# Attention and two feed-forward layers on one core: queries and keys in runs of 2304 bytes, three groups of rows in the down-sampled attention

## The chip, the cores and the metric

The kernel runs on one core of one Trainium2 chip. The metric is the time of one execution in device microseconds (us). Before the change it is 497.21 us, the median of three runs (494.74 to 502.7).

## What is computed

The reference, cut to what matters (batch 2, 8 heads, 576 tokens of 64 values a head; 1152 tokens of 512 values in the layers that follow):

```python
def _attn_ref(q, k, v):
    B, H, S, D = q.shape                       # 2, 8, 576, 64
    factor, Sd, scale = 4, S // 4, 1 / np.sqrt(D)
    q_d = q.reshape(B, H, Sd, factor, D).mean(axis=3)     # k_d, v_d alike
    out_d = sm_attn(q_d, k_d, v_d)             # softmax attention over 144 rows
    out_up = np.repeat(out_d, factor, axis=2)
    mask = np.abs(pos[:, None] - pos[None, :]) < factor
    attn = softmax(np.where(mask, scale * q @ k.T, -1e9))
    return out_up + attn @ v

def reference(...):
    x = attn_out.transpose(0, 2, 1, 3).reshape(B * S, H * D)        # 1152 x 512
    h = x @ w_in;  x = (h * np.tanh(softplus(h))) @ w_out           # 512 -> 2048 -> 512
    g = x @ w_gate; return (silu(g) * (x @ w_val)) @ w_out2         # 512 -> 1536 -> 512
```

## The kernel before

The attention works on pairs of heads: a pair's 2 x 64 values fill the 128 partitions, and there are 8 pairs (4 for each of two batches). `prep` (L476) loads a pair and turns it, `down` (L588) does its down-sampled attention, `load_windows` (L682) loads the value windows of the local attention, and `duo` (L717) does a third of the local attention of two pairs at a time (12 such calls). Its result, split in a high and a low part (`x_hi` on L274 or L272, `x_lo` L813), is the input `xy` of the first layer. The products of the layers run as three single products a chunk (high x high, high x low, low x high: L850, L851, L852, and L1144 to L1146 in the last layer); a product of the first layer for one chunk of 128 features and one third of the tokens is 12 of them.

In `prep` the queries and keys of a pair come by `ld_main` (L495): rows 0 to 511 in runs of 64 values (256 bytes), so that tile `qk` has row 4p + r of both heads on partition p. The last 64 rows of all 8 heads come once a batch by `ld_rem` (L469) into tile `qr`. TensorE turns `qk` in four transposes of 128x128 a matrix (L540) and `qr` in one of 64 rows (L551); ScalarE copies the result out into `qkT` (L557, L561), and VectorE adds four columns each into the down-sampled `qkd` (L568).

In `down` the 144 down-sampled rows of a head stand on 72 partitions in two groups, so that a pair has four groups: four score products (L605), a maximum a head (L610), four exponentials with their sums (L620), four multiplications by the reciprocals (L633 on ScalarE or L635 on VectorE), eight transposes (L644), two copies out (L272), and the products with the values (L656). The sums over the values, `vd` (L523), are GpSimd's.

The local attention of `duo` is: a mask product (L736), scores (L746), maximum and exponentials (L752 to L770), transposes (L776), value products (L789) and the sum with the repeated down-sampled result (L802).

The order of all of it is set by a planner (`Plan.run`). It goes through the program with a cost for each operation and, on each engine, takes the ready operation with the smallest due time; table `STEER` moves the due times of named groups. Where TensorE would have nothing ready, the planner puts a filler product `warm` (L1283, on a tile of zeros) into its order, up to 95 us of its own time. All DMAs are issued by SyncE's queue through one helper (L279), at most 6 under way. Each engine then runs its list in that order, with waits.

Of the kernel before, what the change touches and what calls it, by code (L numbers as in the profile page):

```python
# [62 lines left out]
}  # L63
KB = ()
COLD = 4.0


# [44 lines left out]
class Plan:  # L112
# [17 lines left out]
    def run(self):  # L130
# [10 lines left out]
        while todo:  # L141
            later, ran = [], False
            for e in names:
# [33 lines left out]
                if e == "DVE" and free["POOL"] > now:  # L177
                    d *= self.SHARE
# [1141 lines left out]
```

## Time and profile before

| | |
|---|---|
| runs | 502.7, 494.74, 497.21 us; median 497.21 |
| profiled execution, its own time | 495.21 us |
| its span, first to last instruction | 493.4 us |
| around the span | 1.8 us |
| TensorE busy | 483.1 us, 98% |
| VectorE, ScalarE, GpSimd busy | 327.3, 267.7, 21.5 us |
| mean granted TensorE clock | 0.993 |

A profile is one execution. Busy times count each instruction from start to end, and those of TensorE overlap, so that the time of a product is read from the distance between two starts, or from a piece of the chain of waits, which leaves overlaps out. The chain of waits goes back from the last instruction to what released each step. In views with windows, a DMA share of 1.00 means that all 16 DMA engines had work the whole time (a little above is an artefact of packets that overlap).

### The profile page before, as it was taken

To read this page: it belongs to the slowest core of one execution; us is meant where nothing else is said; L and a number is where in the kernel's file an instruction comes from. 1 tells how busy PE (TensorE), PEld (TensorE's weight loads), DVE (VectorE), ACT (ScalarE), POOL (GpSimd) and SP (SyncE) were. 2 spreads that over 40 slices of the span, in tenths; PEclk is the share of its full clock that TensorE was granted. 3 is DMA by queue.
4 is the path that set the end of the run, shared out by engine and by line. 5 is a ranking of instruction groups with operands and counts; after the bars stand their busy time and mean duration, and the time that the engine had idled before them with its cause. 6 is when DMAs were issued, how large, how long until landed. Compare 5 with 4: busy or idle time off the path is not lost.

```text
span 493.4 us, 9431 instructions
## 1 busy us (share of the span) xinstructions
PE 483.1 (98%) x3857; PEld 454.2 (92%) x3857; DVE 327.3 (66%) x634; ACT 267.7 (54%) x523; POOL 21.5 (4%) x41
## 2 busy tenths in 40 slices
PE   9999799999999999999999999999999999999996
PEld 6777589999999999999999999999998899998885
DVE  4989869639504643865578989798892298872522
ACT  3677668669627733867252775666661485730000
POOL 2333210000000000000000000000000000000000
PEclk9999979999999999999999999999999999999999
DMA  8999996622300640153111051423351042400022
GB/s 169 171 178 187 190 159 181 207 86 86 128 1 0 182 161 1 43 177 123 43 31 55 2 166 48 128 63 111 97 182 62 0 115 101 126 4 0 0 108 85
DMA packets 59993, 48.79 MB, mean 99 GB/s; under 512 B 32430, under 2 KB 55214, under 8 KB 59950
## 3 DMA queue, kind: packets, MB, share of 16 engines
q1 hardware_dynamic: 59950, 48.19, 38.0%
q8 instruction: 30, 0.49, 0.4%
q14 instruction: 13, 0.11, 0.1%
HBM read 45.83 MB, written 2.36 MB: 98 GB/s over the span
## 4 chain that ended last, share of the span: by engine, by line
PE 94%; DMA 4%; issue 1%; DVE 0%; SPq 0%
PE b L850 23%; PE b L852 23%; PE b L851 23%; PE b L1145 5%; PE b L1144 5%; PE b L1146 5%; DMA vw<-in_v_dram 3%; PE warm L1283 2%; PE b L789 2%; DMA qr<-in_k_dram 1%; PE b L540 1%; PE b L746 1%; PE b L605 1%; PE b L656 1%; PE b L776 1%; PE b L644 1%
## 5 line engine op out<-in xcount | busy, mean ns | idle before, releaser
L850 PE MATMUL b<-xy,wt 128*128 128x384 f32 x384 | 129.7, 338 | 0.0
L852 PE MATMUL b<-xy,wt 128*128 128x384 f32 x384 | 128.7, 335 | 0.0
L851 PE MATMUL b<-xy,wt 128*128 128x384 f32 x384 | 128.7, 335 | 0.0
L850 PEld LDWEIGHTS b<-xy,wt 128*128 128x128 f32 x384 | 72.3, 188 | 0.7 <-ACT cw L351 0.4
L851 PEld LDWEIGHTS b<-xy,wt 128*128 128x128 f32 x384 | 72.4, 189 | 0.0
L852 PEld LDWEIGHTS b<-xy,wt 128*128 128x128 f32 x384 | 72.3, 188 | 0.0
L852 PE MATMUL b<-G,wt 128*128 128x384 f32 x192 | 64.7, 337 | 0.0
L850 PE MATMUL b<-G,wt 128*128 128x384 f32 x192 | 64.6, 336 | 0.0
L851 PE MATMUL b<-G,wt 128*128 128x384 f32 x192 | 64.3, 335 | 0.0
L272 ACT ACTIVATE H<-b 128x384 f32<-128x384 f32 x60 | 29.3, 488 | 59.0 <-PE b L852 58.8
L358 DVE SCALAR_TENSOR_TENSOR cw<-raw,cw 128x512 uint32<-128x512 uint32 x68 | 46.5, 685 | 13.2 <-ACT cw L355 12.7
L351 ACT ACTIVATE cw<-raw 128x512 f32<-128x512 int8 x68 | 45.3, 667 | 17.9 <-DVE wt L372 12.5
L372 DVE TENSOR_TENSOR wt<-cw,wt 128x512 fp32r<-128x512 f32 x68 | 46.2, 685 | 5.5 <-ACT wt L272 4.0
L274 DVE CAST wt<-cw 128x512 fp32r<-128x512 f32 x29 | 12.3, 423 | 51.4 <-PE b L851 31.9
L355 ACT ACTIVATE cw<-cw 128x512 int32<-128x512 f32 x68 | 42.7, 628 | 1.0
L1145 PE MATMUL b<-wt,G 128*128 128x512 f32 x108 | 42.3, 392 | 0.0
L1144 PE MATMUL b<-wt,G 128*128 128x512 f32 x108 | 42.2, 391 | 0.0
L1146 PE MATMUL b<-wt,G 128*128 128x512 f32 x108 | 42.1, 390 | 0.0
L851 PEld LDWEIGHTS b<-G,wt 128*128 128x128 f32 x192 | 36.0, 188 | 0.0
L850 PEld LDWEIGHTS b<-G,wt 128*128 128x128 f32 x192 | 36.0, 188 | 0.0
L852 PEld LDWEIGHTS b<-G,wt 128*128 128x128 f32 x192 | 36.0, 188 | 0.0
L965 DVE TENSOR_TENSOR acc<-b,acc 128x384 f32<-128x384 f32 x36 | 19.6, 553 | 23.7 <-PE b L852 23.7
(108 smaller groups left out, 743.0 us busy)
## 6 DMA issues: line engine op xcount, KB each, us to landing
raw<-in_moe_w_out_dram SPq DMA_DIRECT2D x28, 512.0 KB
raw<-in_moe_w_in_dram SPq DMA_DIRECT2D x16, 512.0 KB
raw<-in_moe_w_gate_dram SPq DMA_DIRECT2D x12, 512.0 KB
raw<-in_moe_w_val_dram SPq DMA_DIRECT2D x12, 512.0 KB
vw<-in_v_dram SPq DMA_DIRECT2D x14, 189.0 KB
vq<-in_v_dram SPq DMA_DIRECT2D x8, 288.0 KB
out_dram<-acc SPq DMA_DIRECT2D x9, 256.0 KB
qk<-in_q_dram SPq DMA_DIRECT2D x8, 256.0 KB
```

The costliest lines, as they stand in the source:

```text
L272: ACT.activation(out, in_, AF.Copy)
L351: ACT.activation(cw.make(), raw.tile[:, 8:4104].bitcast(I8).rearrange("p (n b) -> p n b", b=8)[:, :, 0], AF.Prelu, scale=-1.0, bias=-56.0, ...
L355: ACT.activation(cw.tile.bitcast(I32), cw.tile, AF.Prelu, scale=-2.0 ** 27 / SLOPE, bias=-112 * 2.0 ** 27, alpha=SLOPE)
L358: DVE.scalar_tensor_tensor(out=cw.tile.bitcast(U32), in0=raw.tile[:, 0:4096].bitcast(U32).rearrange("p (n b) -> p n b", b=2)[:, :, 1], sca ...
L372: DVE.tensor_tensor(out=wt.tile[:, 1], in0=cw.tile, in1=wt.tile[:, 0].bitcast(F32), op=ALU.subtract)
L850: PE.matmul(out=ps, lhsT=wt_hi, rhs=m_hi, start=first, stop=False, **more)
L851: PE.matmul(out=ps, lhsT=wt_hi, rhs=m_lo, start=False, stop=False, **more)
L852: PE.matmul(out=ps, lhsT=wt_lo, rhs=m_hi, start=False, stop=last, **more)
L965: DVE.tensor_tensor(out=ya, in0=ps.tile[:, 0:n], in1=ya, op=ALU.add)
L1144: PE.matmul(out=ps.tile, lhsT=g[:, 0, tok], rhs=wt[:, 0], start=(f == fs[0]), stop=False)
L1145: PE.matmul(out=ps.tile, lhsT=g[:, 0, tok], rhs=wt[:, 1], start=False, stop=False)
L1146: PE.matmul(out=ps.tile, lhsT=g[:, 1, tok], rhs=wt[:, 0], start=False, stop=(f == fs[-1]))
```

## The change

Four edits in one:

- `ld_main` loads all 576 rows of a pair in runs of nine rows (9 x 64 values, 2304 bytes): partition 64h + n has rows 9n to 9n + 8 of head h. `ld_rem` and tile `qr` are gone.
- `turned` turns row r of the nine by a product of 64x64 with the identity for each head (each on its own 64 partitions), 9 x 2 a matrix. Eight of the nine fill one bank, and the ninth of both matrices shares another. The copies out write with a stride of nine elements. The local scores (`s_local`) now wait for all three copies, where two of three thirds had waited for two.
- `down` has three groups of rows on 128 partitions: the first 80 of the first head's 144 rows, its last 64 beside the first 64 of the second head, and the last 80 of the second head (the products of the first and third group write 128 rows, of which 80 are used). There are two score products of 128 rows and two of 64, a maximum over two groups and one over one, three exponentials, three multiplications, and three transposes for each half of the columns.
- The planner's costs are changed for these operations, VectorE's surcharge beside GpSimd falls on named operations alone (1.5 instead of 1.3 on all), and `STEER` is another table, so that the order on all engines is another.

```diff
 STEER = {
-    ('a', 0, 0, 0, 0, 0, 1): -4.2, ('a', 0, 1, 0, 0, 1, 1): 260.85, ('a', 0, 1, 2, 0, 1, 3): -48.85,
+    ('a', 0, 0, 0, 0, 0, 1): 60.95, ('a', 0, 1, 0, 0, 1, 1): 20.15, ('a', 0, 1, 2, 0, 1, 3): 181.55,
...
-KB = ()
+ROWS = 9
...
+        self.beside = Plan.SHARE if getattr(fn, "__name__", "") in Plan.SHARED else 1.0
...
-    REST, SHARE, REACH, LAND = 0.0, 1.3, 1.5, 0.5
+    REST, SHARE, REACH, LAND = 0.0, 1.5, 1.5, 0.5
+    SHARED = ("norm_l", "x_lo", "lo", "join")
...
-            dma(out=qr.tile[:, i], in_=(q, k)[i][b, :, 512:S].rearrange("h p d -> p h d"))
...
-                    dma(out=t.rearrange("p (r h d) -> p r h d", r=4, h=2), in_=src.rearrange("h (p r) d -> p r h d", r=4))
+                dma(out=qk.tile[:, i], in_=(q, k)[i][b, hs].rearrange("h (p r) d -> (h p) (r d)", r=ROWS))
...
+        def turned(t, z, i, r):
+            for h in range(2):
+                hh = slice(64 * h, 64 * h + 64)
+                PE.matmul(out=t[hh, NR * z:NR * z + NR], lhsT=qk.tile[hh, i, D * r:D * r + D], rhs=ident[hh, hh], start=True, stop=True)
...
-                        PE.transpose(out=t[:, 128 * r:128 * r + 128], in_=qk.tile[:, i, 128 * r:128 * r + 128], identity=ident)
+                for r in range(ROWS - 1):
+                    turned(t, r, i, r)
...
-                PE.transpose(out=t[:, 64 * i:64 * i + 64], in_=qr.tile[:, i, hs].rearrange("p h d -> p (h d)"), identity=ident[:64, :64])
+                turned(t, i, i, ROWS - 1)
...
+                    to = qkT.tile[:, j].rearrange("p (n r) -> p r n", r=ROWS)
+                    ACT.activation(to[:, 0:ROWS - 1] if i < 2 else to[:, ROWS - 1],
...
-            for c in range(2):
-                for h in range(2):
-                    hh = slice(64 * h, 64 * h + 64)
-                    PE.matmul(out=ba[h].tile[0:72, SD * c:SD * c + SD], lhsT=qkd.tile[hh, 0, 72 * c:72 * c + 72],
-                              rhs=qkd.tile[hh, 1, :], start=True, stop=True)
+            for h in range(2):
+                hh = slice(64 * h, 64 * h + 64)
+                PE.matmul(out=ba[h].tile[:, 0:SD], lhsT=t[hh, 64 * h:64 * h + 128], rhs=t[hh, SD:2 * SD], start=True, stop=True)
+            for h in range(2):
+                hh = slice(64 * h, 64 * h + 64)
+                PE.matmul(out=ba[0].tile[hh, SD:2 * SD], lhsT=t[hh, 80 * (1 - h):80 * (1 - h) + 64], rhs=t[hh, SD:2 * SD], start=True, stop=True)
+        rows = ((0, 80), (80, 128), (208, 80))
...
-            for h in range(2):
-                for c in range(2):
-                    ACT.activation(ed.tile[:, h, c], ba[h].tile[0:72, SD * c:SD * c + SD], AF.Exp, bias=md.tile[:, 0, h, c:c + 1],
-                                   scale=1.0 / 16.0, accum_out=md.tile[:, 1, h, c:c + 1])
+            for g in range(3):
+                ACT.activation(ed.tile[:, g], group(g), AF.Exp, bias=md.tile[:, 0, g:g + 1], scale=1.0 / 16.0, accum_out=md.tile[:, 1, g:g + 1])
...
-                for a in range(2):
-                    for c in range(2):
-                        PE.transpose(out=ba[h].tile[0:72, SD * a + 72 * c:SD * a + 72 * c + 72], in_=ed.tile[:, h, c, 72 * a:72 * a + 72],
-                                     identity=ident[:72, :72])
+                for g, (a, n) in enumerate(rows):
+                    PE.transpose(out=ba[h].tile[0:72, a:a + n], in_=ed.tile[0:n, g, 72 * h:72 * h + 72], identity=ident[:n, :n])
...
-            o1.append(add({E_PE: 0.36 if k else 0.48}, s_local(k), pr["evs"][:2 + (u == 2)] + [o_bf] + in_turn[-1:], w,
+            o1.append(add({E_PE: 0.36 if k else 0.48}, s_local(k), pr["evs"] + [o_bf] + in_turn[-1:], w,
```

What the new order does is seen at three places. SyncE's queue at the start of the program, before (`qr` is the tile of the last 64 rows, `qk` that of a pair, `vq` and `vw` the values):

```order
L279 DMA qr_100<-in_q_dram 64x8x64
L279 DMA qr_100<-in_k_dram 64x8x64
L279 DMA qk_134<-in_q_dram 128x8x64
L279 DMA qk_134<-in_k_dram 128x8x64
L279 DMA qk_143<-in_q_dram 128x8x64
L279 DMA qk_143<-in_k_dram 128x8x64
L279 DMA vq_152<-in_v_dram 72x4x256
```

The same queue in the changed kernel:

```order
L281 DMA qk_100<-in_q_dram 128x576
L281 DMA qk_100<-in_k_dram 128x576
L281 DMA qk_132<-in_q_dram 128x576
L281 DMA qk_132<-in_k_dram 128x576
L281 DMA qk_139<-in_q_dram 128x576
L281 DMA qk_139<-in_k_dram 128x576
L281 DMA vq_145<-in_v_dram 72x4x256
```

A pair's queries, which were the third transfer, are the first; each is 128 runs where it was 1024. In all, 106 rows of this queue stand where 111 did.

TensorE at its first down-sampled scores, before (`b` are the banks that products write):

```order
L540 MATMUL b_212<-ident,qk_143 128x128 x4
L551 MATMUL b_219<-ident,qr_100 128x64 x2
L1283 LDWEIGHTS wsrc
L1283 MATMUL warm<-wsrc 128x256
L605 MATMUL b_224<-qkd_198 72x144
L605 MATMUL b_225<-qkd_198 72x144
L605 MATMUL b_224<-qkd_198 72x144
L605 MATMUL b_225<-qkd_198 72x144
L540 MATMUL b_176<-ident,qk_143 128x128 x4
```

And in the changed kernel:

```order
L518 MATMUL b_250<-ident,qk_132 64x64 x16
L518 MATMUL b_268<-ident,qk_132 64x64 x4
L518 MATMUL b_152<-ident,qk_139 64x64 x16
L584 MATMUL b_174<-qkd_231 128x144
L584 MATMUL b_201<-qkd_231 128x144
L587 MATMUL b_174<-qkd_231 64x144 x2
L518 MATMUL b_210<-ident,qk_139 64x64 x16
L518 MATMUL b_250<-ident,qk_139 64x64 x4
```

Four transposes of 128x128 are now 16 products of 64x64, and a filler that stood ahead of the scores is gone. Over the program there are 55 fillers where there were 117 (12 where 26 stood at the start), and the turning is 288 products where it was 64 and 16 transposes.

TensorE just before the first product of the first layer, before (`pt` and `vw` are weights and values of the local attention, `exs` its exponentials, `xy` the layer's input, `wt` its weights):

```order
L789 MATMUL b_219<-pt_435,vw_270 64x32 x2
L789 MATMUL b_212<-pt_435,vw_270 64x32 x2
L776 MATMUL b_224<-ident,exs 128x128 x3
L605 MATMUL b_182<-qkd_234 72x144
L605 MATMUL b_193<-qkd_234 72x144
L850 MATMUL b_225<-xy_82,wt_734 128x384
L851 MATMUL b_225<-xy_82,wt_734 128x384
```

And in the changed kernel:

```order
L626 MATMUL b_174<-ident,ed_377 72x80
L626 MATMUL b_174<-ident,ed_377 72x128
L626 MATMUL b_174<-ident,ed_377 72x80
L717 LDWEIGHTS identb
L717 MATMUL b_210<-masks,identb 128x228
L727 MATMUL b_210<-qkT_209 32x38 x10
L727 MATMUL b_210<-qkT_209 32x35 x2
L831 MATMUL b_201<-xy_82,wt_997 128x384
L832 MATMUL b_201<-xy_82,wt_997 128x384
```

The first layer begins earlier, with more of the attention behind it: 72 of its products stood ahead of the last group of value products (L789) before, and 126 stand ahead of the last group of value products (L770) now. Behind that group both orders hold products of the layers alone.

## Rows read from the trace of the kernel before

**Rows 1.** The page: busy share of the engines, and the chain by engine.

```profile
PE 483.1 (98%) x3857; PEld 454.2 (92%) x3857; DVE 327.3 (66%) x634; ACT 267.7 (54%) x523; POOL 21.5 (4%) x41
...
PE 94%; DMA 4%; issue 1%; DVE 0%; SPq 0%
```

**Rows 2.** Windows: length, busy us of each engine, granted clock, DMA share, GB/s.

```profile
0.00:12.00 12.00, 10.95 (x75) 8.35 (x76) 4.96 (x13) 4.06 (x9) 3.24 (x17) 1.00 0.87 168
12.00:25.00 13.00, 12.07 (x282) 9.46 (x281) 11.70 (x36) 8.88 (x35) 4.25 (x6) 1.00 1.03 172
37.00:50.00 13.00, 12.70 (x321) 10.22 (x321) 12.46 (x36) 10.07 (x37) 4.45 (x6) 1.00 1.18 187
61.00:67.50 6.50, 6.50 (x79) 5.16 (x76) 2.98 (x10) 3.25 (x8) 2.17 (x3) 0.50 1.06 199
95.00:450.00 355.00, 355.00 (x1993) 348.60 (x1992) 239.12 (x407) 201.47 (x325) 0.00 (x0) 1.00 0.26 82
```

**Rows 3.** TensorE's timeline: start, us, instructions, and in brackets the idle time before.

```profile
16.92 0.33 PE L746 MATMUL b<-qkT 64*32 64x38 f32 x14 [0.93 <-issue]
30.71 0.88 PE L789 MATMUL b<-pt,vw 38*64 38x32 f32 x42 [1.03 <-DMA vw<-in_v_dram]
37.26 0.27 PE L551 MATMUL b<-ident,qr 64*128 64x64 f32 x1 [0.26 <-DMA qr<-in_k_dram]
53.83 0.57 PE L746 MATMUL b<-qkT 64*32 64x38 f32 x42 [0.69 <-issue]
59.17 0.59 PE L789 MATMUL b<-pt,vw 38*64 38x32 f32 x25 [2.15 <-issue]
66.19 0.69 PE L850 MATMUL b<-xy,wt 128*128 128x384 f32 x1
84.01 0.33 PE L851 MATMUL b<-xy,wt 128*128 128x384 f32 x1
87.83 0.34 PE L852 MATMUL b<-xy,wt 128*128 128x384 f32 x1
88.09 0.90 PE L789 MATMUL b<-pt,vw 38*64 38x32 f32 x48
```

**Rows 4.** The chain of waits in order of time: start, us, what.

```profile
1.05 5.55 PE warm L1283 x26
6.60 0.47 PE b L540 x4
9.29 0.44 PE b L540 x4
9.73 0.26 PE b L551 x2
10.21 0.65 PE b L605 x8
11.44 0.98 PE warm L1283 x9
37.53 0.37 PE b L644 x4
44.86 0.57 PE b L746 x46
48.86 1.53 PE b L789 x96
```

**Rows 5.** SyncE's queue in its timeline: start, us of issuing.

```profile
0.73 0.74 SPq L279 DMA_DIRECT2D qr<-in_q_dram  x1
2.19 0.63 SPq L279 DMA_DIRECT2D qk<-in_q_dram  x1
```

**Rows 6.** DMA issues: tile, count, KB of each.

```profile
qk<-in_q_dram SPq DMA_DIRECT2D x8, 256.0 KB
qr<-in_q_dram SPq DMA_DIRECT2D x2, 128.0 KB
```

**Rows 7.** Groups of the first 95 us: count, busy us, mean ns.

```profile
L620 ACT ACTIVATE ed<-b,md 72x144 f32<-72x144 f32 x32 | 11.6, 375 | 1.0 <-DVE md L615 0.9
```

More of the change, by code (lines that the diff above doesn't have):

```diff
@@ L177, in run @@
                 if e == "DVE" and free["POOL"] > now:
-                    d *= self.SHARE
+                    d *= o.beside
                 if o.table and table not in SERVED[o.table]:
@@ L264, in us_dma @@
     def us_dma(runs, size, engines=16, issue=None):
-        return [(issue or (0.35 + 0.0003 * runs), runs * (0.0224 if size <= 256 else 0.06 if size <= 1024 else 0.2) / engines, engines)]
+        return [(issue or (0.35 + 0.0003 * runs), runs * (0.0224 if size <= 256 else 0.06 if size <= 1024 else 0.118 if size <= 2304 else 0.2) / engines, engines)]
     def us_mm(n):
@@ L464, in keys @@
         return k0, k1, k0 - (BLK * t - 3)
-    pairs, rems = {}, {}
-    H_ = H
-    def ld_rem(b, i, qr):
-        def f(e):
-            if i == 0:
-                qr.make()
-            dma(out=qr.tile[:, i], in_=(q, k)[i][b, :, 512:S].rearrange("h p d -> p h d"))
-        return f
-    def prep(b, p, w):
-        qk = buf(ld, [128, 2, 512], F32, "qk", 3)
-        plan.at = ("r", b)
-        if p == 0:
-            qr = buf(ld, [64, 2, H_, 64], F32, "qr", 1)
-            l_r = []
-            for i in range(2):
-                l_r.append(plan.add({E_SP: us_dma(64 * H_, 256)}, ld_rem(b, i, qr), l_r, w - 12 - 9.04 + 2.71,
-                                    [] if l_r else [qr], [qr] if l_r else []))
-            rems[b] = (qr, l_r)
-        qr, l_r = rems[b]
+    pairs = {}
+    NR = S // ROWS
+    def prep(b, p, w):
+        qk = buf(ld, [128, 2, ROWS * D], F32, "qk", 3)
         vq = buf(ld, [72, 2, 2, 256], F32, "vq", 2)
@@ L498, in f @@
                     qk.make()
-                t, src = qk.tile[:, i], (q, k)[i][b, hs, 0:512]
-                if b in KB:
-                    dma(out=t.rearrange("p (h f) -> p h f", h=2), in_=src.rearrange("h (p r) d -> p h (r d)", r=4))
-                else:
-                    dma(out=t.rearrange("p (r h d) -> p r h d", r=4, h=2), in_=src.rearrange("h (p r) d -> p r h d", r=4))
+                dma(out=qk.tile[:, i], in_=(q, k)[i][b, hs].rearrange("h (p r) d -> (h p) (r d)", r=ROWS))
             return f
@@ L513, in prep @@
         for i in range(2):
[L514 removed]
+            l_q.append(plan.add({E_SP: us_dma(128, 2304)}, ld_main(i), l_q, w - 12, [] if l_q else [qk], [qk] if l_q else []))
         plan.at = ("v", b, p)
@@ L537, in f @@
                 t = ps[i].make()
-                for r in range(4):
-                    if b not in KB:
-                        PE.transpose(out=t[:, 128 * r:128 * r + 128], in_=qk.tile[:, i, 128 * r:128 * r + 128], identity=ident)
-                        continue
-                    for h in range(2):
-                        a = 256 * h + 64 * r
-                        PE.matmul(out=t[64 * h:64 * h + 64, 128 * r:128 * r + 128], lhsT=qk.tile[:, i, a:a + 64], rhs=ident,
-                                  start=True, stop=True)
+                for r in range(ROWS - 1):
+                    turned(t, r, i, r)
             return f
@@ L641, in f @@
                     ptd.make()
-                for a in range(2):
-                    for c in range(2):
-                        PE.transpose(out=ba[h].tile[0:72, SD * a + 72 * c:SD * a + 72 * c + 72], in_=ed.tile[:, h, c, 72 * a:72 * a + 72],
-                                     identity=ident[:72, :72])
+                for g, (a, n) in enumerate(rows):
+                    PE.transpose(out=ba[h].tile[0:72, a:a + n], in_=ed.tile[0:n, g, 72 * h:72 * h + 72], identity=ident[:n, :n])
             return f
@@ L649, in f @@
             def f(e):
-                copy(e, ptd.tile[:, h].rearrange("p a j -> p (a j)"), ba[h].tile[0:72, 0:2 * SD])
+                copy(e, ptd.tile[:, h], ba[h].tile[0:72, 0:2 * SD])
             return f
@@ L664, in down @@
         o = add({E_PE: 0.68}, score, o_d, w, ba + [ed, md], [qkd])
-        o = [add({"DVE": us_tt(2 * SD)}, mx(h), [o], w, use=[ba[h], md]) for h in range(2)]
+        o = [add({"DVE": us_tt((2 - h) * SD)}, mx(h), [o], w, use=[ba[h], md]) for h in range(2)]
         o = add({"DVE": 0.08}, neg, o, w, use=[md])
-        o = add({"ACT": 1.44}, exps, [o], w, use=ba + [md, ed], table="exp")
+        o = add({"ACT": 1.08}, exps, [o], w, use=ba + [md, ed], table="exp")
         o = add({"DVE": 0.3}, norm, [o], w, use=[md])
         o_e = []
+        x = [add({"ACT": (0.62, 0.31)[h], "DVE": (0.41, 0.21)[h]}, weigh(h), [o], w, use=[md, ed]) for h in range(2)]
         for h in range(2):
-            x = add({"ACT": 0.62, "DVE": 0.41}, weigh(h), [o], w, use=[md, ed])
-            x = add({E_PE: 0.3}, turn(h), [x], w, [] if h else [ptd], [ed, ba[h]] + ([ptd] if h else []))
-            o_e.append(add({"ACT": us_act(2 * SD, True)}, ev(h), [x] + o_e, w, use=[ba[h], ptd]))
+            o = add({E_PE: 0.32}, turn(h), x, w, [] if h else [ptd], [ed, ba[h]] + ([ptd] if h else []))
+            o_e.append(add({"ACT": us_act(2 * SD, True)}, ev(h), [o] + o_e, w, use=[ba[h], ptd]))
         o = add({E_PE: 0.68}, values, o_e + o_v, w, use=[vd, ptd, ba[0]])
```

43 lines of the change are left out of this document (21 added, 22 removed), and 50 rows, old and new, of the table STEER.

## The prediction

> **What bounds the kernel now.** I read the page first. TensorE is busy 98% of the span and 94% of the chain is its own work [rows 1]: whatever is saved must be saved in TensorE's list, as products that go or as time in which it had nothing useful to do. The windows say where that time is [rows 2]. From 95 us on TensorE is busy for all of the 355 us shown, at the full clock, and nothing that the change touches stands there. Before 95 us three things are mixed in: fillers (117 of them, of which the chain shows 26 in the first 5.55 us and 9 in 0.98 us [rows 4]), visible waits of 0.93, 1.03, 0.26, 0.69 and 2.15 us [rows 3], and a stretch from 61 to 67.5 us in which the granted clock is 0.50, the lower level of 1.2 GHz [rows 2]. That stretch follows the wait of 2.15 us, in which TensorE stood still. What TensorE waited for there is mostly data: the DMA share is 0.87 in the first 12 us and 1.03 to 1.18 behind them, at only 168 to 187 GB/s, whereas the stretch from 95 us on moves 82 GB/s with a share of 0.26, which would be 315 GB/s at a full share [rows 2]. The attention's transfers are small runs and fill the queues. VectorE is close behind (11.70 us busy of 13, 12.46 of 13 [rows 2]) and would be the next to end a wait.
>
> So the sum goes over TensorE's list up to the end of the attention, and the rest of the span is taken as it is.
>
> **The change, part by part.**
>
> Transfers. Queries and keys are 16 transfers of 256 KB and 4 of 128 KB [rows 6], together 4608 KB or 4.7 MB. At 172 GB/s with a share of 1.03 [rows 2], 167 GB/s at a full share, they take 28 us of full queues. No row shows runs of 2304 bytes beside small ones; the bounds are 28 us (no gain) and, at 315 GB/s, 15 us. I take 15, because the large runs of [rows 2] are of 1024 and 4096 bytes, on both sides of 2304. These 13 us are not on TensorE's list by themselves. They count through the waits below.
>
> The start. The first transposes begin at 6.60 us [rows 4], 4.4 us after the first pair's queries were issued at 2.19 us [rows 5]. These queries are now first in the queue, at the 0.73 us where `qr` stood [rows 5], so with the same 4.4 us the first products begin at 5.1 us: 1.5 us gained. The 12 fillers that are left there take 5.55 / 26 = 0.213 us each, to 3.6 us, and TensorE then waits 1.5 us. The bounds are 0 and the 3.0 us that 14 fillers took; 1.5 is the middle. The remaining 48 fillers that go took 0.98 / 9 = 0.109 us each [rows 4], 5.2 us. Together -6.7 us. This holds only if nothing else fills the gaps, which is what the next two terms are about.
>
> Turning. What goes: 64 transposes at 0.44 / 4 = 0.11 us, 7.0 us, and 16 at 0.26 / 2 = 0.13, 2.1 us [rows 4]; 9.1 us together. What comes: 288 products of 64x64, which in this number format are two passes each, as four products L605 are "x8" [rows 4]: 576 passes. No row shows such a pass. The nearest is L746, which also works on the two halves of the partitions in turn: 46 passes of 38 columns in 0.57 us, 0.0124 us each [rows 4], or 0.021 for 64 columns. L789 has 0.016 for 32 columns [rows 4], which is 0.032 if the columns count and 0.016 if it is a price of each pass. The lower end is L746's 0.0124 as it stands (7.1 us, -2.0), the upper end a pass as long as half of the 0.13 us of L551, 0.065 (37.4 us, +28.3). I take 0.021, from the row that is alike in its use of partitions: 12.1 us, +3.0 us.
>
> Here a rule speaks against the change: the Trainium skill, page "TensorEngine Tiling (Array Packing)", under "Gotcha 1: PSUM Pressure", says that different row tiles cannot access one PSUM bank at the same time. Both heads' products write one bank, so by that rule they would follow each other, and the term would be that of the second rival below. The trace speaks against it: L850 to L852 take (87.83 - 84.01) / 22 = 0.174 us for 384 columns [rows 3], 0.45 ns a column and so 17 ns for 38, and L746, whose two halves write one bank as well, takes 12.4 ns a pass.
>
> Down-sampled attention. On TensorE 64 transposes L644 at 0.37 / 4 = 0.0925 us [rows 4] become 48 of 80 or 128 columns; at the 0.11 us of the 128-column transposes that is 5.9 against 5.3 us, -0.6. The scores stay at four products of two passes a pair, 0.65 us for eight [rows 4]: 0 (up to +1.9 if a pass with 128 weight columns took 0.11 us). On ScalarE 8 of 32 exponentials with 0.375 us [rows 7] go, 3.0 us, and on VectorE shorter maxima. I cost both at nothing: TensorE's other work covers these engines now. The new wait of the local scores for the third copy also costs nothing as long as TensorE has another pair's work in hand; without that cover it is two small copies on ScalarE for each pair.
>
> Waits. With 13 us less in the queues, the wait of 2.15 us at 57 us should go, and with it the half clock: 6.5 us at 0.50 [rows 2] did the work of 3.2 us, so 3.3 us are lost there. Together -5.4 us. The four other waits, 2.9 us, I leave: with fewer fillers and a first layer that begins earlier, something will be late again, and VectorE is the first candidate. The bounds are 0 and -8.3 us.
>
> Sum: -6.7 + 3.0 - 0.6 - 5.4 = -9.7 us. Span 493.4 - 9.7 = 483.7 us; with the 1.8 us around it 485.5 us. The profiled execution took 495.2 us, 2.0 us under the median of the runs shown (497.2); the forecast is 2.0% under the one and 2.4% under the other. A measurement of this kernel can tell about 2% from no change.
>
> A second reading of the same sum, from the order: 54 more products of the first layer (126 instead of 72) stand ahead of the last group of value products. At 0.174 us they take 9.4 us, which then no longer stand behind it. So the span is 493.4 - 9.4 us plus whatever that group starts later than the 88.09 us of [rows 3]. By the sum it starts at 87.8 us. All that could make the forecast miss shows in that one time.
>
> **The rivals.**
>
> First, the waits stay: VectorE, full in half of the windows, ends the waits where DMA did, or the clock falls to its lower level again. Then the third gain is not there: 493.4 - 6.7 + 3.0 - 0.6 = 489.1, time 490.9 us. For it: 11.70 and 12.46 of 13 us busy. Against it: the change takes work off VectorE, and the longest wait came where transfers were late.
>
> Second, and slower: the two halves do not overlap, and each 64x64 pass loads its weights and streams them alone. At 0.065 us the turning costs +28.3 us: 493.4 - 6.7 + 28.3 - 0.6 - 5.4 = 509.0, time 510.8 us; at 0.050 it is 502.2 us. It decides from 0.038 us a pass on (9.1 + 12.7 us over 576), and 2% slower begins at 0.055. For it: 0.13 us for a product of 64 columns in L551, and the rule above. Against it: L746 and L789, both on quarters or halves of the array, at 12 to 16 ns.
>
> Third, a larger gain: all five waits and the half clock go (-8.3) and the turning costs 0.016 us a pass (+0.1): 493.4 - 6.7 + 0.1 - 0.6 - 8.3 = 477.9, time 479.7 us. For it: 13 us of queue time is more than all waits.
>
> Fourth, the change does not do what it says: runs of 2304 bytes take the queues as long as before. Then neither the start nor the waits gain: 493.4 - 5.2 + 3.0 - 0.6 = 490.6, time 492.4 us. Against it: 315 GB/s for large runs.
>
> **How the numbers follow.** Forecast 0.42, first rival 0.30, second 0.09, third 0.13, fourth 0.06. The range goes from the forecast with the lower end of the turning and without the four waits, 485.5 - 5.0 - 2.9 = 477.6, to the forecast with all waits and L789's 0.032 us, 485.5 + 5.4 + 6.2 = 497.1; rounded to 478 and 498 it leaves out most of the second rival. Faster by over 2% (under 487.3 us) are the third rival and three quarters of the forecast: 0.47 with a little of the first. Slower is most of the second rival, 0.07. The rest, 0.46, is within 2%.
>
> **What would show it.** In the profile of the changed kernel: first turning products at about 5.1 us; 32 passes of one matrix within 0.7 us (over 1.2 us would be the second rival); DMA share under 0.9 in windows between 12 and 50 us; no stretch of half clock between 50 and 70 us; the first product of the first layer by 50 to 56 us instead of 66.19; the last group of value products at 86 to 90 us. A wait of over 1 us on VectorE or ScalarE in TensorE's list behind 40 us would be the first rival, and a last group behind 98 us would make the forecast wrong altogether.

## The result, and the profile after

| | before | after |
|---|---|---|
| median of the runs | 496.95 us (20 runs) | 503.04 us (20 runs) |
| lowest and highest | 489.87 to 502.7 us | 497.31 to 510.29 us |
| ratio to before | | 1.0133, interval 1.0092 to 1.0175 |
| profiled execution | 495.21 us | 497.31 us |
| its span | 493.4 us | 495.5 us |
| its granted clock | 0.993 | 0.993 |

The changed kernel is 1.3% slower. A ratio leaves out runs that lie over 1.5% above the fastest of their kernel, so that it differs a little from the quotient of the two medians. The forecast was 485.5 us, in a range of 478 to 498 us: it had the wrong sign, and the measured time lies above the range.

The page of the profile after, its busy shares and its chain by engine and by line, answers to [rows 1]:

```profile
PE 486.1 (98%) x4275; PEld 457.3 (92%) x4275; DVE 325.0 (66%) x629; ACT 272.7 (55%) x504; POOL 21.5 (4%) x41
...
PE 98%; issue 1%; ACT 1%; DVE 0%
PE b L831 23%; PE b L833 23%; PE b L832 23%; PE b L1126 5%; PE b L1125 5%; PE b L1127 5%; PE b L518 4%; PE b L770 2%; PE warm L1264 2%; PE b L727 1%; PE b L637 1%; PE b L757 1%; PE b L626 1%; PE b L584 1%; PE b L587 1%
```

DMA, which had 4% of the chain, is gone from it. L518, the new turning, has 4% of 495.5 us, some 20 us, where the old one (L540) had 1%. The lines of the new kernel that matter here: L518 turning (on TensorE), L538 ScalarE's copies out of it (the old L557 and L561), L547 VectorE's sums for the down-sampled rows (the old L568), L1264 filler, L584 and L587 scores of the down-sampled attention, L626 its transposes, L727 local scores, L770 value products (the old L789), L831 to L833 products of the first layer (the old L850 to L852).

The windows after, with the columns of [rows 2] (length, busy us of PE, PEld, DVE, ACT, POOL, granted clock, DMA share, GB/s), the last one the half-clock stretch alone:

```profile
0.00:12.00 12.00, 10.93 (x223) 8.69 (x223) 3.72 (x11) 6.38 (x10) 4.78 (x20) 1.00 0.84 232
12.00:25.00 13.00, 10.71 (x277) 8.60 (x279) 8.67 (x28) 8.11 (x26) 2.74 (x4) 1.00 1.02 213
37.00:50.00 13.00, 12.00 (x260) 9.75 (x258) 7.07 (x21) 8.29 (x24) 2.17 (x3) 0.79 0.80 160
50.00:62.00 12.00, 11.85 (x321) 9.22 (x321) 11.21 (x33) 9.70 (x31) 4.46 (x6) 1.00 0.72 183
35.60:42.40 6.80, 6.80 (x97) 5.88 (x93) 3.64 (x8) 2.44 (x7) 2.17 (x3) 0.50 0.74 168
```

The half-clock stretch of the kernel before, in its full length:

```profile
60.90:67.70 6.80, 6.80 (x80) 5.46 (x77) 3.28 (x11) 3.25 (x8) 2.17 (x3) 0.50 1.05 198
```

The transfers did get better: between 37 and 50 us their share is 0.80 where it was 1.18. The runs of 2304 bytes took 15.4 us of the 16 engines (the sum over their packets), which is the 15 us that the prediction took. VectorE, which [rows 2] show nearly full (11.70 and 12.46 of 13 us), now has 8.67 and 7.07 us of work in the same windows: it waits. What VectorE waits for in the first 75 us (us in total, times, longest), before and after:

```profile
DVE qkd L568 <- ACT qkT L561: 3.3, 4, 2.1
```

```profile
DVE qkd L547 <- ACT qkT L538: 10.1, 7, 2.3
```

It waits for ScalarE's copies out of the turning. These, in the same 75 us (count, busy us, mean ns, then the idle time before and who ended it), before and after:

```profile
L557 ACT ACTIVATE qkT<-b 128x512 f32<-128x512 f32 x16 | 9.3, 592 | 9.8 <-PE b L540 9.7
```

```profile
L538 ACT ACTIVATE qkT<-b 128x512 f32<-128x512 f32 x16 | 17.2, 1095 | 13.6 <-PE b L518 13.5
```

Two things got worse here. ScalarE's wait for the turning grew from 9.7 to 13.5 us, and each of the 16 large copies takes 1095 ns instead of 592. And the half clock is not gone: 6.8 us at 0.50, as long as before, only 25 us earlier.

TensorE's timeline after (start, us, instructions, in brackets the idle time before):

```profile
3.72 1.66 PE L518 MATMUL b<-ident,qk 64*64 64x64 f32 x32
17.68 0.64 PE L727 MATMUL b<-qkT 64*32 64x38 f32 x48 [1.21 <-issue]
23.03 0.67 PE L626 MATMUL b<-ident,ed 80*72 80x80 f32 x6 [0.71 <-DVE m L747]
33.71 0.42 PE L770 MATMUL b<-pt,vw 38*64 38x32 f32 x13 [0.85 <-issue]
35.41 2.25 PE L518 MATMUL b<-ident,qk 64*64 64x64 f32 x40
64.14 0.45 PE L831 MATMUL b<-xy,wt 128*128 128x384 f32 x1
99.74 0.90 PE L770 MATMUL b<-pt,vw 38*64 38x32 f32 x48
```

The turning begins at 3.72 us, but the first layer at 64.14 us instead of 66.19 and the last group of value products at 99.74 us instead of 88.09 [rows 3].

In both kernels this stretch can be added up without a remainder, because TensorE is the bound: each product counts from its start to the next one's start, so that a wait behind it and a stretch of half clock are included. 109.0 us of both lists, from the first filler on:

| TensorE, us | before | after |
|---|---|---|
| fillers | 15.9 (117) | 8.3 (55) |
| turning | 10.6 | 21.9 |
| down-sampled scores | 5.7 | 7.9 |
| its transposes and value products | 10.7 | 10.5 |
| mask products, local scores | 11.7 | 12.1 |
| transposes, value products of `duo` | 19.1 | 15.2 |
| products of the first layer | 35.3 (193) | 33.1 (180) |

So at the end of it the changed kernel is 13 products of the first layer behind, at 0.174 us 2.3 us, and that is the 2.1 us by which its span is longer. The fillers gave 7.6 us, the turning took 11.3. The half clock falls on other products than before, and the waits stand behind other ones: of the turning's 21.9 us, 2.1 are lost to the half clock and 0.7 are a wait, and the lower sum of the value products (15.2 for 19.1) is almost all waits and half clock that lie elsewhere now. The account in the section on the prediction takes both out.

The chain of waits has the passes of the turning at full clock (start, us, what), which answers to [rows 4]:

```profile
5.71 1.31 PE b L518 x40
7.35 1.08 PE b L518 x32
9.29 2.25 PE b L518 x72
```

A pass costs 1.31 / 40 = 0.033, 1.08 / 32 = 0.034, 2.25 / 72 = 0.031 us. The forecast had 0.021.

### The profile page after: what moved, and what is told of

It is laid out like the page before. It is cut to its first block, busy times and chain, and to the rows that moved or that the text cites. A ratio compares the mean times of both kernels' runs of the same rounds, so it can differ in the third digit from the quotient of the medians.

```text
span 495.5 us, 10224 instructions
## 1 busy us (share of the span) xinstructions
PE 486.1 (98%) x4275; PEld 457.3 (92%) x4275; DVE 325.0 (66%) x629; ACT 272.7 (55%) x504; POOL 21.5 (4%) x41
## 4 chain that ended last, share of the span: by engine, by line
PE 98%; issue 1%; ACT 1%; DVE 0%
PE b L831 23%; PE b L833 23%; PE b L832 23%; PE b L1126 5%; PE b L1125 5%; PE b L1127 5%; PE b L518 4%; PE b L770 2%; PE warm L1264 2%; PE b L727 1%; PE b L637 1%; PE b L757 1%; PE b L626 1%; PE b L584 1%; PE b L587 1%
## 5 line engine op out<-in xcount | busy, mean ns | idle before, releaser
L831 PE MATMUL b<-xy,wt 128*128 128x384 f32 x384 | 129.7, 338 | 0.0
L833 PE MATMUL b<-xy,wt 128*128 128x384 f32 x384 | 128.6, 335 | 0.0
L831 PEld LDWEIGHTS b<-xy,wt 128*128 128x128 f32 x384 | 72.1, 188 | 0.7 <-ACT ed L604 0.2
L833 PEld LDWEIGHTS b<-xy,wt 128*128 128x128 f32 x384 | 72.1, 188 | 0.0
L833 PE MATMUL b<-G,wt 128*128 128x384 f32 x192 | 64.7, 337 | 0.0
L831 PE MATMUL b<-G,wt 128*128 128x384 f32 x192 | 64.6, 337 | 0.0
L274 ACT ACTIVATE H<-b 128x384 f32<-128x384 f32 x58 | 28.3, 488 | 54.0 <-PE b L833 53.7
L360 DVE SCALAR_TENSOR_TENSOR cw<-raw,cw 128x512 uint32<-128x512 uint32 x68 | 46.9, 693 | 11.0 <-ACT cw L357 10.6
L274 ACT ACTIVATE G<-H 128x1152 fp32r<-128x1152 f32 x14 | 16.0, 1164 | 38.7 <-PE b L1126 21.8
L831 PEld LDWEIGHTS b<-G,wt 128*128 128x128 f32 x192 | 36.0, 188 | 0.0
L833 PEld LDWEIGHTS b<-G,wt 128*128 128x128 f32 x192 | 36.0, 188 | 0.0
```

Source lines behind the costliest of these rows:

```text
L274: ACT.activation(out, in_, AF.Copy)
L360: DVE.scalar_tensor_tensor(out=cw.tile.bitcast(U32), in0=raw.tile[:, 0:4096].bitcast(U32).rearrange("p (n b) -> p n b", b=2)[:, :, 1], sca ...
L831: PE.matmul(out=ps, lhsT=wt_hi, rhs=m_hi, start=first, stop=False, **more)
L833: PE.matmul(out=ps, lhsT=wt_lo, rhs=m_hi, start=False, stop=last, **more)
```

## The experiments

Every ratio is to the kernel before, on the same chip. The changed kernel itself, run once more beside the three experiments that follow it, is the mark for them; the later ones ran on other chips, beside the kernel before alone.

### The changed kernel again

> The changed kernel once more, on the chip on which the variants run. List theory (the turning takes 0.033 us a pass in TensorE's list and all of it is paid): ratio to before 1.00 to 1.02. Clock theory (the median is longer than the profiled run because further stretches of half clock fall into most runs): its runs spread by 3.4 us steps with their mean granted clock, and the fewest such stretches go with the shortest time.

501.85 us, ratio 1.018 (1.0109 to 1.025); span 498.5 us at clock 0.993. Its half clock of 6.8 us lies at 45.7 to 52.5 us. The spread between its six runs goes with the clock: the one with 0.975 took 509.5 us, those with 0.993 took 500.3 and 500.36. But the first profile of the same kernel had 0.993 too, with a span of 495.5 us. The 3.0 us between them are waits: TensorE's add up to 7.3 us here and to 4.3 there, and one wait makes most of it (us in total, times, longest):

```profile
PE b L727 <- issue: 4.1, 1, 4.1
```

### Cheap turning, everything else as it is

```diff
-                for r in range(ROWS - 1):
-                    turned(t, r, i, r)
+                for r in range(4):
+                    PE.transpose(out=t[:, 128 * r:128 * r + 128], in_=qk.tile[:, i, 128 * r:128 * r + 128], identity=ident)
...
-                turned(t, i, i, ROWS - 1)
+                PE.transpose(out=t[:, 128 * i:128 * i + 128], in_=qk.tile[:, i, 448:576], identity=ident)
```

> The changed kernel with its order as it is, but the turning left out: in its place transposes of 128x128 as long as those of before (10 for each pair's matrices instead of 36 products), so the values are not the reference's. List theory: 576 passes at 0.033 us (19.0 us) become 80 transposes at 0.11 us (8.8 us), and the time falls by 8 to 11 us under the changed kernel, to 0.99 to 0.995 of before. Waits theory (the turning is hidden by waits, and the loss is in waits that moved): less than 3 us.

490.23 us, ratio 0.994 (0.9897 to 0.9984), 11.6 us under the changed kernel beside it. The same loads, the same order, the same copies; only TensorE's passes are others, 80 transposes that took 11.6 us of the list instead of 21.9. Its timeline, ScalarE's large copies in the first 75 us, and its stretch of half clock:

```profile
55.22 0.45 PE L831 MATMUL b<-xy,wt 128*128 128x384 f32 x1
90.85 0.90 PE L770 MATMUL b<-pt,vw 38*64 38x32 f32 x48
```

```profile
L538 ACT ACTIVATE qkT<-b 128x512 f32<-128x512 f32 x16 | 17.1, 1109 | 7.5 <-PE b L526 7.3
```

```profile
29.90:36.70 6.80, 6.80 (x59) 4.73 (x58) 4.00 (x9) 4.91 (x12) 2.06 (x3) 0.50 1.02 157
```

Both marks come back by 8.9 us, and ScalarE's wait for the turning falls from 13.5 to 7.3 us. The price of the passes stands on the path, nearly one for one. What does not go with it: TensorE's waits behind the first product still add up to 3.4 us (4.3 in the changed kernel), and the half clock is as long as in the other two.

### The passes doubled

```diff
                 PE.matmul(out=t[hh, NR * z:NR * z + NR], lhsT=qk.tile[hh, i, D * r:D * r + D], rhs=ident[hh, hh], start=True, stop=True)
+                PE.matmul(out=t[hh, NR * z:NR * z + NR], lhsT=qk.tile[hh, i, D * r:D * r + D], rhs=ident[hh, hh], start=True, stop=True)
```

> Each turning product is issued twice, with the same result; order otherwise as in the changed kernel. List theory: another 576 passes at 0.033 us, 16 to 20 us more than the changed kernel. Waits theory: under 8 us, since fillers and waits stand beside them.

518.29 us, ratio 1.0518 (1.0448 to 1.0588): 16.4 us over the changed kernel for 576 more passes, 0.029 us each. With the experiment above this is a slope in both directions.

### The short runs again

```diff
-        qk = buf(ld, [128, 2, ROWS * D], F32, "qk", 3)
+        qk = buf(ld, [128, 2, ROWS, D + 1], F32, "qk", 3)
...
-                dma(out=qk.tile[:, i], in_=(q, k)[i][b, hs].rearrange("h (p r) d -> (h p) (r d)", r=ROWS))
+                dma(out=qk.tile[:, i, :, 0:D], in_=(q, k)[i][b, hs].rearrange("h (p r) d -> (h p) r d", r=ROWS))
```

A row of 65 values on the partition keeps the destination from being one piece, so that each transfer is 1152 runs of 256 bytes.

> The changed kernel with queries and keys landing in rows of 65 values, so that each transfer is 1152 runs of 256 bytes again; order and products as in the changed kernel. Transfer theory (the long runs are worth what the forecast put on them): first products 1 to 3 us later and 5 to 10 us more time. List theory (TensorE's list decides, the transfers had room): within 3 us of the changed kernel.

505.74 us, ratio 1.0251 (1.0187 to 1.0314), 3.9 us over the changed kernel. The DMA queue in the first 62 us (packets, MB, share of 16 engines), of the kernel before, of the changed one and of this one:

```profile
q1 hardware_dynamic: 32007, 11.00, 103.3%
```

```profile
q1 hardware_dynamic: 17511, 11.86, 85.3%
```

```profile
q1 hardware_dynamic: 31684, 10.73, 105.3%
```

The queues are full again and move less, and it costs some 4 us: that is what the long runs are worth here (the two intervals overlap, 1.0109 to 1.025 and 1.0187 to 1.0314, so the size is rough). It lies between the two expectations, and below the 5.4 us of waits and half clock that the prediction drew from the transfers.

### One pass, measured by itself

A small kernel without the attention (its output is zeros, and it leaves out the whole computation) issues rows of products behind fillers at full clock. Two of its loops:

```python
for z in range(24):
    for h in range(2):      # L43: the halves in turn, one bank; L47: a bank each
        PE.matmul(out=banks[0][hs[h], 64 * (z % 8):64 * (z % 8) + 64], lhsT=qk[hs[h], 0, 64 * (z % 9):64 * (z % 9) + 64], rhs=ident[hs[h], hs[h]], start=True, stop=True)
for z in range(48):         # L50: one half only
    PE.matmul(out=banks[3][hs[0], 64 * (z % 8):64 * (z % 8) + 64], lhsT=qk[hs[0], 0, 64 * (z % 9):64 * (z % 9) + 64], rhs=ident[hs[0], hs[0]], start=True, stop=True)
```

> No attention and no layers: TensorE alone, in blocks of 48 like products with 30 fillers between them, and zeros as output. Bank theory (two row tiles in one bank follow each other): 64x64 products of both halves into one bank 0.033 us a pass, into two banks clearly less, 0.015 to 0.022; all on one half 0.033. Streaming theory (a pass of 64 columns costs its columns whatever the bank): 0.029 to 0.035 in all three. Tile theory (64x32 tiles overlap and 64x64 tiles do not): products of 32 weight columns at 0.012 us for 38 moving columns and at 0.015 to 0.020 for 64. Scores with 128 weight columns and 144 moving columns 0.10 to 0.115 us a pass, with 72 weight columns 0.08.

TensorE's timeline of it (start, us from the first start to the last end, shapes of weight tile and operand, count of passes):

```profile
14.62 3.01 PE L43 MATMUL b<-ident,qk 64*64 64x64 f32 x96
20.95 3.02 PE L47 MATMUL b<-ident,qk 64*64 64x64 f32 x96
27.27 5.81 PE L50 MATMUL b<-ident,qk 64*64 64x64 f32 x96
36.39 1.06 PE L55 MATMUL b<-qk 64*32 64x38 f32 x96
40.77 1.54 PE L60 MATMUL b<-ident,qk 64*32 64x64 f32 x96
57.12 5.40 PE L70 MATMUL b<-ident,qk 128*128 128x128 f32 x48
75.14 6.15 PE L78 MATMUL b<-qk 64*128 64x144 f32 x96
84.61 6.10 PE L82 MATMUL b<-qk 64*64 64x144 f32 x96
```

A block's time is counted to the start of the filler behind it (17.57 us for L43, 23.89 for L47, 33.01 for L50, 37.39 for L55, 42.24 for L60, 62.36 for L70). So a pass of 64 columns is 59.8 ns when all go to one half (L50), 30.7 ns when two halves take turns (L43), and 15.4 ns when four tiles of 64x32 do (L60). A pass is thus equally long on its tile in all three, some 60 ns, and as many run beside each other as there are different tiles in turn. L55 is the form of the row that the prediction scaled, L746: four tiles, 10.4 ns. The turning has two. None of the three theories came out as written: one bank or two is the same, one half alone is twice as long, and tiles of 64x64 overlap as those of 64x32 do. Against transposes of 128x128 (L70, 109 ns), 72 passes of 30.7 ns a pair replace 10 transposes, 2.2 against 1.1 us. A product with 128 weight columns is no dearer than one with 64 when its like stand in a row (L78, L82). The count of tiles is not the whole price, though: the value products L789 also go to four tiles in turn (two halves of the rows, two of the columns), with 32 columns, and take 16 ns a pass [rows 4], as much as L60 with 64 columns. What sets that was not tried.

### Every filler twice

```diff
             PE.matmul(out=wtile[:, 0:256], lhsT=wsrc[:, 0:128], rhs=wsrc[:, 0:256], start=True, stop=True)
+            PE.matmul(out=wtile[:, 0:256], lhsT=wsrc[:, 0:128], rhs=wsrc[:, 0:256], start=True, stop=True)
```

> The changed kernel with every filler issued twice, so 110 products where 55 are. Clock theory (fewer fillers are why the clock falls oftener): the mean granted clock of its runs rises from 0.985 to that of the kernel before (0.990) or above, and the time grows by less than the 6 us that 55 fillers take, or falls. List theory alone: mean clock as in the changed kernel, and 4 to 7 us more time.

505.23 us, ratio 1.016 (1.0103 to 1.0217). The clock of its runs is 0.995 in the mean, against 0.985 over 26 runs of the changed kernel and 0.987 over the 11 runs of before beside it. That is what the clock theory wanted. More fillers go with a higher clock, then, but what they give back they cost: the ratio stays near that of the changed kernel (1.0133 and 1.018 on other chips).

### Four groups of rows again

The changed kernel with the `down` of the kernel before, in two orders: with the table as it stands the planner puts in 130 fillers, and with a table made for it 76 (the changed kernel has 55).

> The changed kernel with the down-sampled attention of before (four groups of 72 rows); its order is the planner's for these operations with the same table, so the order moves as well. If the three groups are worth something (fewer exponentials on ScalarE): 2 to 6 us slower than the changed kernel. If they cost what their scores cost on TensorE (1.5 us): 1 to 3 us faster.

> The changed kernel with the four groups of rows of the kernel before in its down-sampled attention, this time with an order planned for it (76 fillers instead of 55, against 130 in the attempt before). If the loss lies in the turning and the groups are worth little, it comes within 3 us of the changed kernel: a span of 494 to 501 us, a ratio of 1.00 to 1.02. If the three groups with their 128 weight columns are part of the loss: a span under 493 us, a ratio under 0.997. If the three groups gain what the attempt before showed: a ratio over 1.025.

In this order they took 513.73 us, ratio 1.0375 (1.0281 to 1.047), and 507.94 us, ratio 1.0225 (1.0118 to 1.0332). The first lies in no range that was expected, and says little, since 75 fillers more are in it. The second has its span, 498.5 us, in the range of the first theory, and its ratio just above it. In the second, L600 is the old exponential; before it, the changed kernel's:

```profile
L604 ACT ACTIVATE ed<-b,md 128x144 f32<-128x144 f32 x24 | 8.7, 375 | 2.5 <-DVE md L600 2.5
```

```profile
L600 ACT ACTIVATE ed<-b,md 72x144 f32<-72x144 f32 x32 | 11.5, 370 | 3.1 <-DVE md L595 3.1
```

Three groups do save their 3 us of ScalarE, and nothing shows them as the main cause of the loss: without them the time is not lower in either order. Whether they gain the half per cent between 1.018 and 1.0225 can't be told; the intervals overlap and the orders differ.

### The right price in the planner

```diff
-            o = plan.add({E_PE: (0.56 if i < 2 else 0.15)}, t_main(i) if i < 2 else t_rem,
+            o = plan.add({E_PE: (1.06 if i < 2 else 0.27)}, t_main(i) if i < 2 else t_rem,
```

with a table found for it, 20 fillers.

> The changed kernel itself with one difference: the costs of the turning products in the planner are 1.06 and 0.27 us instead of 0.56 and 0.15, and the steering table is one found for these costs, so that the start holds 20 fillers instead of 55 and another order. The turning passes are as dear as in the changed kernel. If the order was made for a price that is too low and that is what costs, 35 fillers at 0.109 to 0.15 us (4 to 5 us) go and waits behind the passes go with them: a span of 487 to 492 us, a ratio of 0.985 to 0.997. If the price of the passes alone makes the loss, the fillers' place is taken by waits: a span of 494 to 498 us, a ratio of 1.005 to 1.02.

505.6 us, ratio 1.0268 (1.019 to 1.0346), slower than both theories. Waits took the fillers' place, as the second theory said, and more, 10.7 us instead of 4.3; the largest:

```profile
22.78 0.71 PE L638 MATMUL b<-ptd,vd 72*64 72x144 f32 x8 [1.89 <-issue]
37.47 0.98 PE L728 MATMUL b<-qkT 64*32 64x35 f32 x47 [3.46 <-issue]
44.58 0.65 PE L638 MATMUL b<-ptd,vd 72*64 72x144 f32 x6 [1.77 <-issue]
```

The planner priced the turning at half of what it takes; but that this made the order bad is not borne out by this one other order.

### Four quarters instead of two halves

If tiles in turn are what counts, queries and keys on different halves give four tiles of 64x64. Two attempts: queries on the lower and keys on the upper 64 partitions (two half-width transfers, the code below), and queries as they were with the keys' heads swapped by two transfers of 64 partitions. Both need a fourth bank and share one new order with 72 fillers.

```diff
-                dma(out=qk.tile[:, i], in_=(q, k)[i][b, hs].rearrange("h (p r) d -> (h p) (r d)", r=ROWS))
+                dma(out=qk.tile[64 * i:64 * i + 64], in_=(q, k)[i][b, hs].rearrange("h (p r) d -> p h (r d)", r=ROWS))
...
+            for i, h in ((0, 0), (1, 1), (0, 1), (1, 0)):
+                ii = slice(64 * i, 64 * i + 64)
+                PE.matmul(out=ps[p0 + i].tile[64 * h:64 * h + 64, NR * z:NR * z + NR], lhsT=qk.tile[ii, h, D * r:D * r + D],
+                          rhs=ident[ii, ii], start=True, stop=True)
```

> The changed kernel with queries on the lower and keys on the upper half of the partitions (still in runs of 2304 bytes, both heads side by side), so that the turning products go to four quarters of the array in turn instead of two; in this form the order of the start had to be planned anew (72 fillers instead of 55). Tiles in flight: four tiles in turn cost 15.4 ns a pass in the small kernel, so 576 passes take 8.9 us instead of the 21.9 us of the changed kernel's list, and some 13 us less in the list, minus 2 to 3 us for the 17 more fillers, gives a span of 485 to 489 us, a ratio of 0.975 to 0.99. Rival, 64x64 tiles overlap no more than two at a time whatever their number (30.7 ns a pass, 17.7 us): a span over 493 us, a ratio of 0.995 to 1.01. In the profile, 32 passes in a row take 0.5 us by the first and 1.0 us by the second.

> The attempt with four quarters again, in the same order on TensorE, with the queries landing on all 128 partitions as in the changed kernel and the keys in two transfers of 64 partitions that swap the two heads, so that the four products of a row again go to four quarters. In the attempt before, 64 passes in a row took 1.16 us (18 ns each) but the runs of 2304 bytes took 164 ns each at the median, against 93 in the changed kernel, and the list stood 17 us more than before in waits and half clock. If the loss there came from the way in which its transfers land on 64 partitions, the runs come back towards 93 ns (at least for the queries), the waits of 3.9 and 3.8 us go, and the span is 485 to 492 us, a ratio of 0.98 to 0.995. If the four quarters themselves or this order cost what was lost, the span stays over 500 us, a ratio over 1.015.

511.66 us, ratio 1.0348 (1.0272 to 1.0424), and 508.75 us, ratio 1.0318 (1.0277 to 1.0358): both are slower than the changed kernel (1.0133 and 1.018). The first lies in neither of its two ranges, the second in the rival's. The timeline of the second attempt:

```profile
19.68 1.16 PE L523 MATMUL b<-ident,qk 64*64 64x64 f32 x64
34.62 0.56 PE L628 MATMUL b<-ident,ed 128*72 128x128 f32 x2 [3.44 <-issue]
55.28 0.32 PE L772 MATMUL b<-pt,vw 38*64 38x32 f32 x7 [1.85 <-issue]
```

A pass fell to 1.16 / 64 = 0.018 us, so the tiles in turn hold inside the kernel too. But its transfers got worse, which the queue of its first 62 us shows, and the clock with them:

```profile
q1 hardware_dynamic: 16052, 11.34, 95.6%
```

```profile
37.00:50.00 13.00, 12.33 (x220) 9.20 (x217) 7.70 (x21) 6.72 (x15) 4.34 (x6) 0.50 1.05 159
```

A run of 2304 bytes took 148 ns at the median (164 in the first attempt) against 93 in the changed kernel, and the mean clock of the runs fell to 0.969. In the two other orders with the loads of the changed kernel (the right price, and four groups in the second order) the median is 95 and 93 ns, so that a new order alone does not make the runs longer. For the time, two causes stay unseparated: the transfers onto 64 partitions, and an order of its own. Neither attempt beats the kernel before, and no other version did that computes the whole result.

## Why the prediction was wrong

The list of 109.0 us once more, with the waits and the loss by the half clock (an estimate, half of the time that lies in it at 0.50) taken out of the products and put in rows of their own:

| us, after less before | forecast | measured |
|---|---|---|
| turning | +3.0 | +8.7 (10.3 to 19.0) |
| down-sampled attention | -0.6 | +1.9 (scores +1.7) |
| fillers, with the earlier start | -6.7 | -7.7 |
| visible waits | -2.1 | -0.8 (5.1 to 4.3) |
| half clock | -3.3 | 0 (3.4 in both) |
| span | -9.7 | +2.1 |

What the table leaves out, the local attention (-0.6) and the first layer for an equal count of products (+0.8), nearly cancels. Two terms make most of the miss of 11.8 us: the turning 5.7, the waits with the half clock 4.6.

**The turning, +3.0 us predicted, +8.7 measured (+11.3 in the list, with the half clock and the wait that fell on it).** This is the step that failed first. "I take 0.021, from the row that is alike in its use of partitions": L746 is alike in its rows, but its weight tiles are 64x32, four of them in turn, and the turning has two. By itself a pass is 30.7 ns with two and 15.4 with four; in the kernel it is 31 to 34 ns, and 38 over all 576 with what the half clock and a wait add. The price was inside the bounds (0.0124 to 0.065) and close to the 0.032 that L789 gave by columns, but that nearness is luck: L789 has four tiles in turn and 32 columns, and twice the columns happens to give the same factor as half the tiles. The halves do overlap, so the second rival, which took 0.065 and began to decide at 0.038, did not happen, though its direction did. That the price is on the path is shown from both sides: -11.6 us with cheap passes, +16.4 us with doubled ones.

**The waits, -5.4 us predicted, -0.8 measured.** This is the second step that failed. The visible waits after the first product are 4.3 us instead of 5.1, and the half clock is as long as before. It begins at 35.6 us, behind a wait of 0.85 us that ends at 33.7, where it began at 60.9 behind one of 2.15 that ended at 59.2. The first rival (the waits stay, or the clock falls again) came true in its second half, not by VectorE being full: VectorE has less to do (39.4 us in the first 62, against 49.8) and waits for ScalarE, and ScalarE for the turning. It is not one cause with the first term. With the cheap turning, 11.6 us where the forecast had 12.1, waits of 3.4 us and the whole half clock stay; that kernel took 490.2 us, where the forecast said 485.5 and the first rival 490.9. Why the waits stay is open. One candidate was in no term of the sum: ScalarE's large copies out of the turning, which now write every ninth element, take 1095 ns instead of 592, 8 us more over the 16, and they do so in every version that was run, so that no run tells their worth.

The upper end of the range was made of just these two errors, L789's price and no gain from the waits, 497.1 us. The profiled execution took 497.31; the median of all runs lies above it.

**The start and the fillers, -6.7 predicted, -7.7 measured.** The direction and size hold. The products began at 3.72 us, not 5.1: 3.0 us after their queries were issued at 0.73, and not 4.4 us after. In the experiment with short runs they began at 4.57 us, so the long runs give 0.85 us; the rest may be the `qr` that stood ahead in the queue.

**The down-sampled attention, -0.6 predicted, +1.9 measured.** Its scores are four products of two passes a pair as before, but of two forms. Before, after, and with four groups again (the second order):

```profile
22.97 0.71 PE L605 MATMUL b<-qkd 64*72 64x144 f32 x8
```

```profile
15.35 0.52 PE L584 MATMUL b<-qkd 64*128 64x144 f32 x4
15.80 0.46 PE L587 MATMUL b<-qkd 64*64 64x144 f32 x4
```

```profile
28.20 0.71 PE L585 MATMUL b<-qkd 64*72 64x144 f32 x8
```

To the next product's start, at 23.61, 16.20 and 28.85 us, a pair's scores take 0.64, 0.85 and 0.65 us: 1.6 us more over eight pairs. I had the bound at +1.9 for dear 128-column weights; these are not dear by themselves (L78 and L82 in the small kernel). The time goes at the change of form: the last pass of L584 and the first of L587 lie 0.21 us apart, where passes of one form follow at 0.06 to 0.08.

**The second reading held.** The span is 493.4 - 9.4 us plus what the last group starts later: 99.74 - 88.09 = 11.65, together 495.6; measured 495.5. The text gave 98 us as the point from which the forecast is wrong altogether. Of the other signs: 32 passes took 1.08 us (0.7 wanted, over 1.2 the second rival), and 1.66 in the first group, at the start, where a filler takes 0.21 us and not 0.11; the DMA share was under 0.9 only from 37 us on; the first layer began at 64.14 us, not by 56. No half clock lies between 50 and 70 us, and that sign misled: it lies earlier.

**The rest of the way to the median.** The profiled executions differ by 2.1 us, the medians by 6.1. Of 26 runs of the changed kernel and 52 of before, those with a clock of 0.99 or more have medians of 500.3 us (10 runs) and 492.7 us (26 runs), the others 504.0 and 499.4; the means of the clock are 0.985 and 0.989. So at like clock the loss is some 5 to 8 us, of which the pair of profiles shows less than most pairs of runs would. The two profiles of the changed kernel differ by 3.0 us at one clock, by their waits. The lower mean clock, 0.004 of some 500 us, is worth about 2 us (an estimate). That it comes from the 62 missing fillers is supported by the doubled fillers, which went with a higher clock, and not shown.

**The rule.** The Trainium skill's page "TensorEngine Tiling (Array Packing)", "Gotcha 1: PSUM Pressure", which the prediction weighed, says that different row tiles cannot access one bank at the same time. It does not slow these products: a pass takes 30.7 ns with one bank and with two. The prediction's doubt of it was right, and its rival lost its reason, though not its direction. The working of that doubt was too mild: it set L746's 12.4 ns against 17 ns for 38 columns, from products of the first layer in another number format (fp32r). In the turning's format 64 columns on one tile take 59.8 ns, 0.93 ns a column and not 0.45, so that 38 would take some 36 ns (an estimate). L746's 12.4 ns is a third of that: more than two passes run side by side there, and the turning has only two tiles.

## What to carry to other kernels

Price a small product by the number of different tiles that take turns, not by the rows it uses: with fp32 passes of 64 columns, one tile gave one pass at a time, two gave two, four gave four, and a row of the trace should only be scaled to a form with as many tiles of the same size (the value products, at 16 ns for 32 columns on four tiles, show that columns alone do not scale either). Transfers that get shorter are worth what their wait was, which a full queue does not tell (some 4 us here, of 13 us of queue time by the prediction's sum); where their consumer is the engine that bounds the kernel, a dearer consumer eats it. Follow the new layout through every engine that touches it: here the copies out nearly doubled, and no term had them. And before a rearrangement of a load, replace the dear consumer by a cheap stand-in, as the cheap turning does here: one run tells what the price is worth.

## What the hardware showed that was not expected

- Passes of 64 columns overlap by the count of tiles: 59.8, 30.7 and 15.4 ns a pass with one, two and four tiles in turn; with two it is the same whether they write one bank or two.
- ScalarE's copy of 128x512 values out of a bank took 592 ns when it read the bank with a stride and wrote one piece, and 1095 ns when it read it in order and wrote every ninth element.
- The step from four score passes with 128 weight columns to four with 64 took 0.21 us, where passes of one form follow at 0.06 to 0.08.
- Runs of the same 2304 bytes took 93 ns at the median onto 128 partitions, and 148 and 164 ns in the two kernels that land some or all of them on 64 (120, 156 and 165 ns in the mean).
- The stretch at half clock was 6.8 us long in the kernel before, after, and in the changed kernel's second run, at 60.9, 35.6 and 45.7 us: the change did not shorten it, and its place differs between two runs of one kernel.
